# Attention and experts on one core: products with v spread by a table of shares, VectorE's low part of exp read from PSUM, new times for a pair's steps

## The chip, the core and the metric

One NeuronCore of a Trainium2 chip. Times are device microseconds (us) of one execution. TensorE (PE; its weight loads are PEld) multiplies, VectorE (DVE) and ScalarE (ACT) read PSUM and SBUF, GpSimd (POOL) works in SBUF, and SyncE (SP) issues the DMAs. The metric is the median time of a run.

## The reference

```
q_pool = q.reshape(B, H, S // 2, 2, D).mean(axis=3)        # B 2, H 8, S 1152, D 64: 576 pooled queries per head
scores = q_pool @ k^T / sqrt(D);  attn = softmax(scores);  x = attn @ v
out = sum_e p[:, e] * (relu(x @ w1[e]) @ w2[e])            # 1152 rows of 512, 4 experts of 1024
result = ((out @ m1) * (out @ m2)) @ m3 @ mo
```

All in float32. Two outputs of 576 rows and 16 heads in all: 8 pairs of heads.

## The kernel before, in words

**The work of a pair.** Attention goes pair by pair (`i` 0 to 7, heads `s` 0 and 1). For each of the 9 chunks `c` of 128 keys a head takes four score products into a PSUM tile `s` of two banks (L494; two such tiles in all), two passes of exp on ScalarE (L503 `whole`: exp in float32 into an SBUF tile `p`, of which there are four; L510 `hi`: exp in float16 into `ph`), and a subtraction `pl = p - ph`, the low part (`lo`, L515), on GpSimd or VectorE. A head's 135 products with v (`av`, L538 and L540: 5 row blocks, 9 chunks, and ph with v's high part, ph with v's low part, pl with v's high part) run while the next head's scores are made, into one PSUM tile that all heads share. Then `dn` and `x` (L544 to L555) divide and free that tile.

**The next pair's preparation** runs beside it. k is transposed (`kt`, L238; its two parts use the PSUM tiles w0, of two banks, and w1, of one), and cut into `kab` (ScalarE) and `kl` (VectorE). q is pooled on GpSimd (`qp`, L209 and L212), transposed (`qt`, w0) and cut into `qh`, `QZ` and `ql`. For each block of rows a product `mp` (L349, its first two thirds into w0, its last third into w1) and two reductions `mx` on VectorE (L352) find the row maxima: five blocks for head 0, four for head 1. `mf` joins them, `mr` (w1) turns them, `mh` and `ml` cut them, and DMAs place them in the score operand. v gets a scale (`vm`, `vt` in w1, `va` to `vd`, `vs`, `cxp`), and is cut into `vt` high (L470, ScalarE) and low (L474, VectorE). After pairs 3 and 7, `prx` (L464) takes the scale of a whole batch into the experts' shares. The last pair has the first expert's work beside it in place of a next pair's.

**What sets the order.** Every step is put on an agenda with a time written out by hand, and the agenda, sorted, is the order of every engine's instructions. One unit is one chunk; a pair takes 18. The times are offsets in constants at the top: `EX`, `HI`, `LO` for `whole`, `hi` and `lo` after a chunk's scores, `AV0` and `AVN` for the start and length of a head's products with v (spread evenly), `MX0` and `MX1` for the maxima, `KT`, `QT` for the turns of k and q, `TURN` and `ME` for the maxima's turn, `VL` for v's low part, `PQ` for the pooling. An engine runs its instructions in that order, and each waits for what it reads and for the buffer that it writes. PSUM is full: w0 and w1 pass from step to step, so a product waits for the VectorE or ScalarE instruction that read the tile last.

Of the kernel before, what the change touches and what calls it, by code (L numbers as in the profile page):

```python
# [9 lines left out]

TURN = 0.95
KH = 0.15
KL_ = 0.6
QH_ = 0.85
QL_ = 0.5
M0 = 0.4
M1 = 0.05
M2 = 0.6
HI_DVE = (4,)
LO_DVE = ((1, 4), ())  # L20
EX = 0.85
HI = 1.15
LO = 2.1
AV0 = 1.2
AVN = 7.65
VH = 0.5
VL = 3.35
VL0 = -5.5
VR = 4.85
VT = (0.75, 0.8)  # L30
VE = (6.5, 6.75)
PQ = 2.9
PQS = 1.0
WARM = 39
WARM_K = 10
WARM_N = 5
WARM_E = 27
VH0 = 1.5
FIRST = (0.3, 1.4, 2.3, 4.5)
NEAR = 0.0  # L40
LATER = 0
KT = (3, 4)
QT = 5
MX0 = (7, 8, 10, 11, 13)
MX1 = (14, 16, 17, 19)
ME = 0.15
LAST = ((2, 4, 6), (1, 5, 7))
SW = 130
W0 = 123.5
# [14 lines left out]
F32 = mybir.dt.float32  # L64
# [4 lines left out]
AF = mybir.ActivationFunctionType  # L69
ALU = mybir.AluOpType  # L70
# [12 lines left out]
def tile_kernel(ctx: ExitStack, tc: tile.TileContext, q, k, v, dp, w1, w2, mw1, mw2, mw3, mwo, out):  # L83
    nc = tc.nc
    B, H, S, D = q.shape
    P = 128
# [112 lines left out]
    def at(t, f, *args):  # L199
        agenda.append((t, len(agenda), f, args))  # L200
# [281 lines left out]
    def plan_scores(i, s, t):  # L482
        for c in range(NC):
            st = {}

            def pe(c=c, st=st):
                if c == 0:
                    pht[i, s] = ph_p.tile([P, NC, T], F16, tag="ph", name=f"ph{i}_{s}")
                    plt[i, s] = ph_p.tile([P, NC, T], F16, tag="pl", name=f"pl{i}_{s}")
                ps = st["s"] = ps_s.tile([P, 2, 512], F32, tag="s", name=f"s{i}_{s}_{c}")  # L490
                cs = slice(c * P, (c + 1) * P)
                for a, b, first in ((K1, Q1, True), (K2, Q2, False)):
                    for n in range(2):
                        mm(  # L494
                            ps[:, n, :HALF], a[s][:, cs], b[s][:, n * HALF : (n + 1) * HALF],
                            start=first, stop=not first,
                        )

            two = lambda ap: ap.rearrange("p (n t) -> p n t", n=2)

            def whole(c=c, st=st):
                p32 = st["p"] = p32_p.tile([P, T], F32, tag="p32", name=f"p32_{i}_{s}_{c}")
                nc.scalar.activation(out=two(p32), in_=st["s"][:, :, :HALF], func=AF.Exp, scale=SCORE)  # L503

            def hi(c=c, st=st):
                o = pht[i, s][:, c, :]
                if c in HI_DVE:
                    nc.vector.tensor_copy(o, st["p"])
                else:
                    nc.scalar.activation(out=two(o), in_=st["s"][:, :, :HALF], func=AF.Exp, scale=SCORE)  # L510

            def lo(c=c, st=st):
                on_dve = LO_DVE[s] if i < NPAIR - 1 else LAST[s]
                eng = nc.vector if c in on_dve else nc.gpsimd
                eng.tensor_tensor(out=plt[i, s][:, c, :], in0=st["p"], in1=pht[i, s][:, c, :], op=ALU.subtract)  # L515

            at(t + c, pe)
            at(t + c + EX, whole)
            at(t + c + HI, hi)
            at(t + c + LO, lo)  # L520

    def plan_av(i, s, t, span):
        b, h = PAIRS[i]
        xd = slice((h + s) * D, (h + s + 1) * D)
        xo = X[b][:, :, xd]
        st = {}

        def one(j, c, n):
            if (j, c, n) == (0, 0, 0):
                st["t"] = ps_a.tile([P, NB + 1, D + 1], F32, tag="a", name=f"av{i}_{s}")
            o = j * P if j < NB else T - P
            p = (pht, pht, plt)[n][i, s][:, c, o : o + P]
            t = st["t"]
            if n == 1:
                mm(t[:, j, 0:D], p, vt[s][:, c, 0:D], start=False, stop=False)  # L538
            else:
                mm(t[:, j, :], p, vt[s][:, c, D:], start=(c == 0 and n == 0), stop=(c == NC - 1 and n == 2))  # L540

        def out_of():
            dn = tiny.tile([P, NB + 1], F32, tag="dn", name=f"dn{i}_{s}")
            nc.vector.tensor_scalar(  # L544
                out=dn, in0=st["t"][:, :, D], scalar1=PS * EPS, scalar2=vs[i][:, s : s + 1],
                op0=ALU.add, op1=ALU.mult,
            )
            nc.vector.reciprocal(out=dn, in_=dn)
            n = NB if b else NB + 1
            nc.vector.tensor_tensor(  # L550
                out=xo[:, :n], in0=st["t"][:, :n, :D], in1=dn[:, :n].unsqueeze(2).to_broadcast([P, n, D]), op=ALU.mult
            )
            if b:
                r = slice(64, 128)
                nc.vector.tensor_scalar(  # L555
                    out=XT[r, xd], in0=st["t"][r, NB, :D], scalar1=dn[r, NB:], scalar2=None, op0=ALU.mult
                )

        todo = [(j, c, n) for j in range(NB + 1) for c in range(NC) for n in range(3)]
        for k, x in enumerate(todo):  # L560
            at(t + span * k / len(todo), one, *x)
        at(t + span + OUT, out_of)


# [643 lines left out]
```

## Time and profile before

| | |
|---|---|
| median of 3 runs | 877.14 us (876.72 to 877.37) |
| profiled execution | 875.1 us, of which the span from the first to the last instruction is 873.3 us |
| PE busy in the span | 833.9 us, 95% |
| DVE, ACT, POOL busy | 643.4, 406.3, 307.0 us |
| attention after the first half pair (43 to 283 us) | PE 222.2 of 240 us, DVE 204.3, ACT 182.6, POOL 174.5 |

The profile gives one execution. Busy time of an engine is the time in which it has an instruction at work. A gap on PE is put down to the instruction that released it. A time on PE from one group's start to the next group's start is what the group costs there, since matmuls overlap.

### The profile page before, as it was taken

What the parts mean: (1) busy time and instruction counts of PE and PEld (TensorE: products, weight loads), DVE (VectorE), ACT (ScalarE), POOL (GpSimd) and SP (SyncE); (2) the same over time, 40 slices, a digit from 0 to 9 for tenths busy, and PEclk for the clock granted to TensorE, in tenths of its full rate; (3) what the DMA queues carried; (4) which work ended last, traced back from release to release, by engine and by line L of the source; (5) the groups of instructions that cost most, each with busy time, mean ns of one, the idle gap of its engine ahead of it and who ended that gap; (6) DMA issues with size and microseconds to landing.
All of it is one profiled execution on the core that took longest, in us unless ns stands there. A gap on an engine that the chain in (4) does not pass through costs nothing.

```text
span 873.3 us, 16029 instructions
## 1 busy us (share of the span) xinstructions
PE 833.9 (95%) x6388; PEld 597.2 (68%) x6388; DVE 643.4 (74%) x1098; ACT 406.3 (47%) x729; POOL 307.0 (35%) x268
## 2 busy tenths in 40 slices
PE   7799899999889999999999989999999999998998
PEld 5688788888767655555455545555557889988887
DVE  6788988888886566877898988986677865996000
ACT  2677777787685533333344444332214333334111
POOL 4588778777753000000112111101110235667200
PEclk9699999999999999999999999999999999999999
DMA  7666757765440022122222233321110321220011
GB/s 184 161 146 148 173 121 156 163 146 123 112 116 27 25 73 73 51 71 73 73 76 75 92 97 97 97 73 49 49 49 1 107 86 47 78 93 25 13 49 48
DMA packets 59833, 76.74 MB, mean 88 GB/s; under 512 B 23480, under 2 KB 41264, under 8 KB 59760
## 3 DMA queue, kind: packets, MB, share of 16 engines
q1 hardware_dynamic: 59760, 75.73, 32.8%
q8 instruction: 50, 0.82, 0.4%
q14 instruction: 23, 0.19, 0.1%
HBM read 51.92 MB, written 2.36 MB: 62 GB/s over the span
## 4 chain that ended last, share of the span: by engine, by line
PE 64%; DVE 26%; DMA 4%; issue 3%; ACT 1%; SPq 1%; POOL 0%; DVEq 0%; ACTq 0%; POOLq 0%
PE up L678 19%; PE dn L718 18%; PE o L1163 6%; DVE mx L352 5%; PE wf L1115 5%; PE gt L1146 5%; PE s L494 4%; PE mp L349 3%; DVE cv_a L818 2%; DVE vt L474 2%; PE av L540 2%; DVE cv_a L812 2%; DVE cv_a L815 2%; DMA rw<-in_moe_w 1%; DVE w L653 1%
## 5 line engine op out<-in xcount | busy, mean ns | idle before, releaser
L718 PE MATMUL dn<-w,h 128*128 128x512 f16 x840 | 186.4, 379 | 0.0
L515 POOL TENSOR_TENSOR pl<-p,ph 128x576 f16<-128x576 f32 x124 | 164.2, 1338 | 49.2 <-ACT ph L510 38.2
L678 PEld LDWEIGHTS <-w 128*128 128x128 f16 x1152 | 111.7, 98 | 76.0 <-issue 1.6
L718 PEld LDWEIGHTS <-h 128*128 128x128 f16 x840 | 81.6, 98 | 93.2
L684 ACT ACTIVATE up<-up 128x320 f32<-128x320 f32 (+1 forms) x96 | 45.7, 476 | 171.8 <-PE up L678 171.8
L352 DVE TENSOR_REDUCE mx<-mp 128x1 f32<-128x768 f32 (+1 forms) x144 | 101.8, 751 | 21.6 <-PE mp L349 21.2
L494 PE MATMUL s<-Q,K 128*128 128x288 f32 x576 | 113.5, 323 | 2.1 <-ACT ph L510 1.2
L678 PE MATMUL up<-xB,w 128*128 128x320 f16 x768 | 110.5, 299 | 0.6 <-DVE xB L775 0.5
L503 ACT ACTIVATE p<-s 128x576 f32<-128x576 f32 x144 | 93.6, 650 | 34.8 <-PE s L494 29.6
L689 DVE TENSOR_TENSOR h<-up,h 128x320 f16<-128x320 f32 (+1 forms) x94 | 50.8, 551 | 55.8 <-ACT h L685 55.5
L678 PE MATMUL up<-xA,w 128*128 128x512 f16 x384 | 89.1, 379 | 0.6 <-DVE xA L775 0.6
L494 PEld LDWEIGHTS s<-Q,K 128*128 128x128 f32 x576 | 86.6, 198 | 2.8 <-ACT ph L510 1.5
L825 POOL TENSOR_TENSOR cv_x<-cv_x,cv_a 128x512 f32<-128x512 f32 x24 | 30.8, 1284 | 154.3 <-DVE cv_x L822 154.3
L540 PE MATMUL av<-vt,ph 128*128 128x65 f16 x720 | 82.9, 194 | 0.8 <-DVE XT L555 0.6
L540 PE MATMUL av<-vt,pl 128*128 128x65 f16 x720 | 82.9, 196 | 0.2 <-DVE pl L515 0.2
L510 ACT ACTIVATE ph<-s 128x576 f16<-128x576 f32 x128 | 82.6, 645 | 0.0
L538 PE MATMUL av<-vt,ph 128*128 128x64 f16 x720 | 82.2, 194 | 0.0
L825 POOL TENSOR_TENSOR r<-r,cv_a 128x512 f32<-128x512 f32 x16 | 20.4, 1278 | 159.4 <-DVE r L822 159.4
L540 PEld LDWEIGHTS <-ph 128*128 128x128 f16 x720 | 67.1, 99 | 6.9 <-DVE XT L555 1.8
L538 PEld LDWEIGHTS <-ph 128*128 128x128 f16 x720 | 67.0, 97 | 5.7 <-issue 2.3
L540 PEld LDWEIGHTS <-pl 128*128 128x128 f16 x720 | 67.0, 98 | 3.9 <-issue 1.1
L349 PE MATMUL mp<-kab,QZ 128*128 128x384 f32 x216 | 58.3, 377 | 7.4 <-DVE mx L352 4.0
(153 smaller groups left out, 1355.9 us busy)
## 6 DMA issues: line engine op xcount, KB each, us to landing
rw<-in_moe_w SPq DMA_DIRECT2D x64, 512.0 KB
K<-kab SPq DMA_DIRECT2D x32, 288.0 KB
rk<-in_k SPq DMA_DIRECT2D x16, 288.0 KB
rv<-in_v SPq DMA_DIRECT2D x8, 576.0 KB
Q<-qh SPq DMA_DIRECT2D x32, 144.0 KB
K<-kl SPq DMA_DIRECT2D x16, 288.0 KB
rq<-in_q SPq DMA_DIRECT2D x8, 512.0 KB
rw<-in_moe_w_out SPq DMA_DIRECT2D x8, 512.0 KB
```

What stands on the lines that cost most here:

```text
L349: mm(ps[:, n, :PC], QZ[:, o : o + P], KAB[i][:, sl], start=True, stop=True)
L352: nc.vector.tensor_reduce(out=mx[i, s][:, j, g : g + 1], in_=st.pop((j, g))[:, :, :PC], axis=AX.XY, op=ALU.max)
L494: mm(ps[:, n, :HALF], a[s][:, cs], b[s][:, n * HALF : (n + 1) * HALF], start=first, stop=not first,)
L503: nc.scalar.activation(out=two(p32), in_=st["s"][:, :, :HALF], func=AF.Exp, scale=SCORE)
L510: nc.scalar.activation(out=two(o), in_=st["s"][:, :, :HALF], func=AF.Exp, scale=SCORE)
L515: eng.tensor_tensor(out=plt[i, s][:, c, :], in0=st["p"], in1=pht[i, s][:, c, :], op=ALU.subtract)
L538: mm(t[:, j, 0:D], p, vt[s][:, c, 0:D], start=False, stop=False)
L540: mm(t[:, j, :], p, vt[s][:, c, D:], start=(c == 0 and n == 0), stop=(c == NC - 1 and n == 2))
L678: mm(p, w[:, a, c, fc * P : (fc + 1) * P], x[b][:, c, lo - o : hi - o], start=(c == 0 and a == b), stop=(c == KD - 1 and a == 1),)
L718: mm(p, hid[n][a][:, fc, t * P : (t + 1) * P], w[:, b, fc, :], start=(fc == 0 and a == b), stop=(fc == 1 and a == 1),)
L825: nc.gpsimd.tensor_tensor(out=x, in0=x, in1=a.bitcast(F32), op=ALU.add)
L1163: mm(p, gt[c][:, a, t * P : (t + 1) * P], wf[c][:, b, lo:hi], start=(m == 0), stop=(m == 23))
```

## The change

Three things. First, `lo` on VectorE no longer reads `p` from SBUF: for these chunks ScalarE makes `hi` first, then writes float32 exp over the scores in PSUM, and VectorE subtracts from there. These are now chunk 2 of head 0 of a pair (before: chunks 1 and 4), and in the last pair the same chunks as before, 2, 4, 6 and 1, 5, 7. The copy that made `hi` of chunk 4 on VectorE is gone; ScalarE makes it like the others. Second, a head's products with v are spread over its time by a table of shares for eight equal parts of it. Third, nearly all constants have new values.

```diff
-HI_DVE = (4,)
-LO_DVE = ((1, 4), ())
-EX = 0.85
-HI = 1.15
-LO = 2.1
-AV0 = 1.2
-AVN = 7.65
+LO_DVE = ((2,), ())
+EX = 0.49
+HI = 1.01
+LO = 1.19
+LOV = 1.09
+AV0 = 1.09
+AVN = 7.58
+AVW = ((1.0, 0.1, 0.85, 0.35, 1.25, 0.35, 1.15, 2.95), (1.0, 1.5, 0.7, 1.3, 1.5, 0.5, 0.5, 1.0))
...
-VL = 3.35
+VL = 2.56
...
-KT = (3, 4)
+KT = (3.05, 3.05)
...
-            def whole(c=c, st=st):
-                p32 = st["p"] = p32_p.tile([P, T], F32, tag="p32", name=f"p32_{i}_{s}_{c}")
-                nc.scalar.activation(out=two(p32), in_=st["s"][:, :, :HALF], func=AF.Exp, scale=SCORE)
+            on_dve = c in (LO_DVE[s] if i < NPAIR - 1 else LAST[s])
+
+            def whole(c=c, st=st, on_dve=on_dve):
+                x = st["s"][:, :, :HALF]
+                if on_dve:
+                    o = x
+                else:
+                    st["p"] = p32_p.tile([P, T], F32, tag="p32", name=f"p32_{i}_{s}_{c}")
+                    o = two(st["p"])
+                nc.scalar.activation(out=o, in_=x, func=AF.Exp, scale=SCORE)
...
-                if c in HI_DVE:
-                    nc.vector.tensor_copy(o, st["p"])
+                nc.scalar.activation(out=two(o), in_=st["s"][:, :, :HALF], func=AF.Exp, scale=SCORE)
...
+                if on_dve:
+                    nc.vector.tensor_tensor(out=two(o), in0=st["s"][:, :, :HALF], in1=two(h), op=ALU.subtract)
                 else:
...
-            at(t + c + EX, whole)
-            at(t + c + HI, hi)
-            at(t + c + LO, lo)
+            at(t + c + (HI if on_dve else EX), whole)
+            at(t + c + (EX if on_dve else HI), hi)
+            at(t + c + (LOV if on_dve else LO), lo)
...
+        share = AVW[s] if span == AVN else (1,) * 8
+        ends = [sum(share[:n]) / sum(share) for n in range(9)]
         for k, x in enumerate(todo):
-            at(t + span * k / len(todo), one, *x)
+            y = k / len(todo)
+            n = max(m for m in range(8) if ends[m] <= y)
+            at(t + span * (n + (y - ends[n]) / (ends[n + 1] - ends[n])) / 8, one, *x)
```

Three places where it moves instructions. The first is VectorE from the last maxima of pair 4 to the next pair's k, before the change; the numbers in a name are pair, head and step, and the last one counts tiles.

```order
L352 TENSOR_REDUCE mx4_1_2575<-mp4_1_3_1_2734 128x1
L368 TENSOR_REDUCE mf4_1_2773<-mx4_1_2575 128x4
L369 TENSOR_REDUCE mf4_1_2773<-mx4_0_2359 128x1
L515 TENSOR_TENSOR pl4_0_2712<-p32_4_0_1_2759,ph4_0_2711 128x576
L474 SCALAR_TENSOR_TENSOR vt0_120<-rv4_1913,vs4_2345,vt0_120 128x9x64
L393 TENSOR_TENSOR ml4_1_2823<-mr4_1_2811,mh4_1_2817 5x128
L244 TENSOR_TENSOR kl5_2800<-kt5_0_2801,kab5_2799 128x768
```

And the same stretch of VectorE after it.

```order
L353 TENSOR_REDUCE mx4_1_2546<-mp4_1_3_1_2729 128x1
L369 TENSOR_REDUCE mf4_1_2762<-mx4_1_2546 128x4
L370 TENSOR_REDUCE mf4_1_2762<-mx4_0_2365 128x1
L475 SCALAR_TENSOR_TENSOR vt0_120<-rv4_1927,vs4_2357,vt0_120 128x9x64
L520 TENSOR_TENSOR pl4_0_2709<-s4_0_2_2765,ph4_0_2708 128x576
L394 TENSOR_TENSOR ml4_1_2829<-mr4_1_2807,mh4_1_2824 5x128
L245 TENSOR_TENSOR kl5_2810<-kt5_0_2811,kab5_2809 128x768
```

The low part of chunk 1, from SBUF, stood ahead of v's low part; now that of chunk 2, from PSUM, stands behind it, and `ml` still follows both.

The second place is TensorE at the turn of the maxima and of k in the same pair, before; 15 more products with v, the scores of chunk 4 and then `kt5_1` follow.

```order
L494 MATMUL s4_0_3_2794<-Q2_0_128,K2_0_124 128x288 x2
L238 MATMUL kt5_0_2801<-ident_64,rk5_2322 128x128 x6
L540 LDWEIGHTS pl3_1_2424
L540 MATMUL av3_1_2744<-vt1_121,pl3_1_2424 128x65
L540 LDWEIGHTS ph3_1_2423
L540 MATMUL av3_1_2744<-vt1_121,ph3_1_2423 128x65
L385 MATMUL mr4_1_2811<-ident_64,mf4_1_2773 5x128
L538 LDWEIGHTS ph3_1_2423
L538 MATMUL av3_1_2744<-vt1_121,ph3_1_2423 128x64
```

And the same place after.

```order
L495 MATMUL s4_0_3_2801<-Q2_0_128,K2_0_124 128x288 x2
L386 MATMUL mr4_1_2807<-ident_64,mf4_1_2762 5x128
L239 MATMUL kt5_0_2811<-ident_64,rk5_2292 128x128 x6
L239 MATMUL kt5_1_2818<-ident_64,rk5_2292 128x128 x3
L546 LDWEIGHTS ph3_1_2420
L546 MATMUL av3_1_2737<-vt1_121,ph3_1_2420 128x64
```

`kt5_1` writes the tile w1 that `ml4_1` has to read out first. Between `mr4_1` and it stood 16 products with v and the scores of chunk 4; now only `kt5_0` stands there, and those products and the scores come behind it.

The third place is VectorE in the middle of a pair, from the third to the fifth block of the next pair's maxima, before.

```order
L352 TENSOR_REDUCE mx5_0_2969<-mp5_0_2_1_3059 128x1
L352 TENSOR_REDUCE mx5_0_2969<-mp5_0_3_0_3088 128x1
L352 TENSOR_REDUCE mx5_0_2969<-mp5_0_3_1_3091 128x1
L474 SCALAR_TENSOR_TENSOR vt1_121<-rv4_1913,vs4_2345,vt1_121 128x9x64
L352 TENSOR_REDUCE mx5_0_2969<-mp5_0_4_0_3151 128x1
L352 TENSOR_REDUCE mx5_0_2969<-mp5_0_4_1_3154 128x1
L508 CAST ph4_1_3033<-p32_4_1_4_3175 128x576
L366 TENSOR_REDUCE mf5_0_3195<-mx5_0_2969 128x5
```

And after.

```order
L353 TENSOR_REDUCE mx5_0_2974<-mp5_0_2_1_3055 128x1
L475 SCALAR_TENSOR_TENSOR vt1_121<-rv4_1927,vs4_2357,vt1_121 128x9x64
L353 TENSOR_REDUCE mx5_0_2974<-mp5_0_3_0_3093 128x1
L353 TENSOR_REDUCE mx5_0_2974<-mp5_0_3_1_3096 128x1
L353 TENSOR_REDUCE mx5_0_2974<-mp5_0_4_0_3130 128x1
L353 TENSOR_REDUCE mx5_0_2974<-mp5_0_4_1_3133 128x1
L367 TENSOR_REDUCE mf5_0_3164<-mx5_0_2974 128x5
```

v's low part moved ahead of the fourth block's reductions, and the copy of chunk 4 is gone.

## Rows read from the trace of the kernel before

**Rows 1.** Window of the attention: busy us of each engine, granted clock, DMA

```profile
43.00:283.00 240.00, 222.19 (x3065) 192.21 (x3064) 204.33 (x370) 182.62 (x321) 174.46 (x148) 0.99 0.56 131
```

**Rows 2.** Windows by pair, from one pair's first maxima product to the next's

```profile
99.63:131.28 31.65, 28.30 (x387) 24.70 (x387) 28.24 (x51) 23.62 (x43) 24.22 (x22) 1.00 0.62 141
...
160.92:190.58 29.66, 28.12 (x387) 24.61 (x387) 25.72 (x48) 23.71 (x43) 24.34 (x22) 1.00 0.64 150
190.58:220.43 29.85, 28.02 (x387) 24.55 (x387) 25.88 (x49) 23.75 (x43) 24.02 (x22) 1.00 0.59 129
```

**Rows 3.** Waits of PEld in the pair 160.92:190.58: us, times, longest

```profile
PEld kt L238 <- DVE ml L393: 0.9, 1, 0.9
PEld mp L349 <- PE s L494: 0.5, 1, 0.5
PEld vt L425 <- PE av L540: 0.4, 1, 0.4
```

**Rows 4.** The chain through the same pair: start us, us, what

```profile
165.65 0.20 PE av L540
...
165.88 0.06 PE av L540 x2
...
168.70 1.71 DVE vt L474
...
174.33 0.61 PE s L494 x4
174.93 0.53 PE mp L349 x3
...
179.71 1.43 DVE mx L352 x2
...
182.21 2.25 DVE vt L474
184.46 0.21 DVE ml L393
...
184.71 0.56 PE kt L238 x3
```

**Rows 5.** VectorE's groups in that pair: busy us, mean ns, idle before

```profile
L352 DVE TENSOR_REDUCE mx<-mp 128x1 f32<-128x768 f32 x9 | 8.6, 954 | 2.6 <-PE mp L349 2.6
L474 DVE SCALAR_TENSOR_TENSOR vt<-rv,vs,vt 128x576 f16<-128x576 f32 x2 | 4.0, 2020 | 0.0
L515 DVE TENSOR_TENSOR pl<-p,ph 128x576 f16<-128x576 f32 x2 | 1.7, 860 | 0.0
L508 DVE CAST ph<-p 128x576 f16<-128x576 f32 x2 | 0.9, 447 | 0.0
L295 DVE TENSOR_TENSOR ql<-qt,qh 128x576 fp32r<-128x576 f32 x1 | 0.7, 737 | 0.0
```

**Rows 6.** Timeline of ScalarE, the two passes over a chunk: start us, us

```profile
163.00 0.65 ACT L503 ACTIVATE p<-s 128x576 f32<-128x576 f32 x1 [1.04 <-PE s L494]
163.54 0.65 ACT L510 ACTIVATE ph<-s 128x576 f16<-128x576 f32 x1
```

**Rows 7.** Timeline of POOL and PE in the first pair; then a window of PE there

```profile
31.14 1.28 POOL L515 TENSOR_TENSOR pl<-p,ph 128x576 f16<-128x576 f32 x1
...
34.15 1.09 PE L291 MATMUL qt<-ident,qp 128*128 128x128 f32 x4 [1.25 <-POOL pl L515]
...
36.00:38.00 2.00, 1.17 (x5) 0.50 0.91 206
```

**Rows 8.** Timeline of VectorE and PE at the eighth pair's first maxima

```profile
220.87 2.44 DVE L464 TENSOR_SCALAR prx<-pr,cxi 128x16 f32<-128x16 f32 x2
...
224.35 1.15 PE L349 MATMUL mp<-kab,QZ 128*128 128x384 f32 x3 [1.96 <-DVE mx L352]
```

**Rows 9.** Timeline of VectorE and PE in the last pair

```profile
244.31 2.35 DVE L611 TENSOR_REDUCE wm<-rw 128x1 f32<-128x1024 f32 x2
...
246.84 0.28 PE L385 MATMUL mr<-ident,mf 128*5 128x128 f32 x1 [0.84 <-DVE mf L369]
```

More of the change, by code (lines that the diff above doesn't have):

```diff
@@ L9 @@
 from concourse.masks import make_identity
[L11 to L14, printed above, removed]
+TURN = 1.03
+KH = 0.59
+KL_ = 0.22
+QH_ = 0.35
 QL_ = 0.5
-M0 = 0.4
-M1 = 0.05
-M2 = 0.6
-HI_DVE = (4,)
-LO_DVE = ((1, 4), ())
-EX = 0.85
-HI = 1.15
-LO = 2.1
-AV0 = 1.2
-AVN = 7.65
-VH = 0.5
-VL = 3.35
[L28 to L33, printed above, removed]
+M0 = 0.2
+M1 = 0.01
+M2 = 0.39
+LO_DVE = ((2,), ())
[6 more added lines that the diff above has]
+AVW = ((1.0, 0.1, 0.85, 0.35, 1.25, 0.35, 1.15, 2.95), (1.0, 1.5, 0.7, 1.3, 1.5, 0.5, 0.5, 1.0))
+VH = 0.15
+VL = 2.56
+VL0 = -4.21
+VR = 4.92
+VT = (0.27, 0.8)
+VE = (6.01, 6.93)
+PQ = 1.67
+PQS = 1.3
 WARM = 39
@@ L38 @@
 VH0 = 1.5
-FIRST = (0.3, 1.4, 2.3, 4.5)
+FIRST = (0.71, 1.14, 2.3, 4.68)
 NEAR = 0.0
 LATER = 0
-KT = (3, 4)
[L43 to L46, printed above, removed]
+KT = (3.05, 3.05)
+QT = 4.89
+MX0 = (7, 8, 10, 11.72, 13.01)
+MX1 = (14, 16, 17, 18.92)
+ME = 0.07
 LAST = ((2, 4, 6), (1, 5, 7))
@@ L499, in plan_scores, with lo @@
             two = lambda ap: ap.rearrange("p (n t) -> p n t", n=2)
-            def whole(c=c, st=st):
-                p32 = st["p"] = p32_p.tile([P, T], F32, tag="p32", name=f"p32_{i}_{s}_{c}")
-                nc.scalar.activation(out=two(p32), in_=st["s"][:, :, :HALF], func=AF.Exp, scale=SCORE)
+            on_dve = c in (LO_DVE[s] if i < NPAIR - 1 else LAST[s])
[7 more added lines that the diff above has]
+                nc.scalar.activation(out=o, in_=x, func=AF.Exp, scale=SCORE)
             def hi(c=c, st=st):
                 o = pht[i, s][:, c, :]
-                if c in HI_DVE:
-                    nc.vector.tensor_copy(o, st["p"])
-                else:
[L510 to L515, printed above, removed]
+                nc.scalar.activation(out=two(o), in_=st["s"][:, :, :HALF], func=AF.Exp, scale=SCORE)
+            def lo(c=c, st=st, on_dve=on_dve):
+                o, h = plt[i, s][:, c, :], pht[i, s][:, c, :]
+                if on_dve:
+                    nc.vector.tensor_tensor(out=two(o), in0=st["s"][:, :, :HALF], in1=two(h), op=ALU.subtract)
+                else:
+                    nc.gpsimd.tensor_tensor(out=o, in0=st["p"], in1=h, op=ALU.subtract)
             at(t + c, pe)
-            at(t + c + EX, whole)
-            at(t + c + HI, hi)
-            at(t + c + LO, lo)
+            at(t + c + (HI if on_dve else EX), whole)
+            at(t + c + (EX if on_dve else HI), hi)
+            at(t + c + (LOV if on_dve else LO), lo)
     def plan_av(i, s, t, span):
```

## The prediction

> **What bounds the kernel now.** I read the window of the attention first, then those by pair, then the waits of one pair and the chain through it. In the first the reader is to see that TensorE is the busiest engine, but that in the attention it stands idle for 17.8 us of 240 (240 - 222.2) [rows 1]. The experts' work behind it keeps its instructions and their order, so what can move lies in the attention and the start: at most some 18 us, 2%.
>
> The windows by pair give the period: 29.66 us in the first batch, 29.85 in the second, and 31.65 where `prx` falls [rows 2]. Within a period TensorE waits several times, and nearly always for VectorE: 0.9 us at `kt` for `ml`, 0.4 at `vt`, 0.5 at the first maxima product (put down to PE; what comes late there is `cxp`, which frees w1) [rows 3]. VectorE is busy for 25.72 of 29.66 us, ScalarE for 23.71, GpSimd for 24.34 [rows 2]. The chain shows the same: from 179.71 to the second part of `kt` at 184.71 it stays on VectorE, through reductions, `pl`, 2.25 us of v's low part and `ml` [rows 4]. So a pair is bound by TensorE and VectorE in turns, and TensorE's own work does not change. The question is which of its waits go and which come.
>
> **The change, part by part.**
>
> *VectorE's work.* Per pair it loses two copies of 0.447 and two low parts of 0.860 from SBUF, and gains one low part with one operand in PSUM [rows 5]: no row shows that form. The nearest is `ql`, the same subtraction of 576 columns with PSUM as first operand, at 0.737; the other end is the SBUF form's 0.860. I take 0.74, or 0.7 from start to start. VectorE loses 2.61 - 0.74 = 1.9 us per pair. [...]
>
> *ScalarE and GpSimd.* ScalarE makes `hi` of chunk 4 in both heads: two more passes of 0.65 per pair [rows 6], 25.0 of 29; no row shows exp written into PSUM, and I price it like the same pass into SBUF. GpSimd makes 17 low parts instead of 16, at 1.28 [rows 7]: 25.6 of 29. Both have over 5 us idle per pair now [rows 2], and that idle time hides them, so they cost nothing. Without that cover, ScalarE's 1.3 us would go onto each pair.
>
> *The tile held longer.* Chunk 2's PSUM tile is now freed by VectorE, not ScalarE, and the scores of chunk 4 want it. On TensorE those scores come behind `kt`'s second part, which waits for `ml`, and `ml` stands behind this low part on VectorE. So the hold costs nothing of its own. What stands behind it is `ml`, and that is counted below.
>
> *The order of a pair.* I split the period 160.92 to 190.58 at two events: the head's first product with v at 165.65, and `kt`'s second part at 184.71 [rows 4]. That makes 4.73 + 19.06 + 5.87 us.
>
> First part, now 4.73: VectorE does two blocks of maxima (1.43 each) and then `dn` to `x`. TensorE comes to the second block 6 products earlier (12 instead of 18, 0.03 each), but its tile is only free when the first reduction (0.954) is over [rows 5]. I count 0.1 off (0 to 0.2).
>
> Second part, now 19.06. TensorE's own work is 135 products at 0.03 = 4.1, eight scores at 0.61 = 4.9, five maxima products at 0.53 = 2.65, and `mr`, one small product, at 0.1 by estimate: 11.7 us to the last maxima product [rows 4]. Waits come on top: v's low part (1.71) now stands ahead of the fourth block's reductions, and fewer products lie between the blocks (15 and 8, before 35 and 18). TensorE therefore waits about 0.4 at the fifth block and 0.4 at the first of the other head: 12.5. Before, VectorE began the last block's reductions 14.06 after the part's start (179.71 - 165.65); now it is 12.5 + 0.55 for the product = 13.05, because 35 products instead of 14 lie between the last two blocks, and `dn` to `x` fit there. From there: reductions 1.43, `mf` 0.2, v's low part 2.25, `pl` 0.7, `ml` to `kt` 0.25 [rows 4] = 4.85, `pl` being the price above. Sum 17.9, so 1.15 off. v's low part took 1.71 and 2.25 in this one pair, so it has those two prices; I take the long one, as it is the one in this place. With 1.71 another 0.5 goes. In the second batch `x` has a further instruction for the odd rows, which puts back some 0.4; over three pairs of each batch that is 0.2. So 0.95 off (0.4 to 1.5).
>
> Third part, now 5.87, of which 0.9 are waits at `vt` and at the first maxima product [rows 3], both behind the copy, the second low part and their neighbours on VectorE. These have left this place, so I count the waits as gone: 5.0 us of work. The scores of chunk 4 (0.61) and 16 products (0.5) come into this part from the second: 6.1, so 0.2 more.
>
> Together 0.1 + 0.95 - 0.2 = 0.85 off per pair, times six periods, from the first maxima product of the second pair's scores to that of the eighth's: 5.1 us.
>
> *The stretch of prx.* TensorE waits 1.96 us there at the eighth pair's maxima, and about as long at the fourth's, in the period that is 2 us longer than the others [rows 2, 8]. `prx` waits on nothing that moves: 0 (0.5 either way for each).
>
> *The start.* `qt` of the second pair began at 34.15 after 1.25 us of waiting [rows 7]. Its tile is freed by a reduction that stood behind `vm` on VectorE and now stands ahead of it; the pooled q now comes behind two low parts on GpSimd (1.28 each) instead of one. About 1 us earlier, of which I keep 0.5, since the later turns here wait for other steps (0 to 1).
>
> *The last pair.* `mr` waited 0.84 us because `mf` stood behind two reductions of the expert's weights (2.35) [rows 9]. Now `mf` stands ahead: 0.84 off. Against it, two low parts that wait for ScalarE move up among the expert's first steps; for it, the last one moves out of the way of `wa`. I count 0.8 off (2 off to 1 more).
>
> Sum: 5.1 + 0.5 + 0.8 = 6.4. The profiled execution took 875.1 us (span 873.3 and 1.8 around it), 2.0 less than the median of the runs, 877.14. 875.1 - 6.4 = 868.7 on its scale, **870.7 us** as a median.
>
> **The rivals.**
>
> *The waits only move (no change).* The new waits in the middle of a pair are twice what I count and `kt` waits longer, 0.7 per pair in all. For it: the table of shares puts fewer products between the maxima there, though VectorE needs 1.43 per block. Against it: VectorE has 1.9 us less to do. Then 0.15 per pair and the smaller terms stay: 0.9 + 1.3 = 2.2 off, 874.9, and with those at nothing 876.2.
>
> *Slower: the low part from PSUM holds up `ml`.* Place: between v's low part and `ml` on VectorE. It waits for ScalarE's second pass over chunk 2. ScalarE has v's high part and six passes to do from the end of the head's products on, some 0.8 + 6 x 0.54 = 4.0 us, as two passes start 0.54 apart [rows 6]; VectorE comes to it 4.4 us after the last maxima product (0.55 + 1.43 + 0.2 + 2.25), and the products end 0.6 before that. So ScalarE has about a microsecond in hand. Beyond that each microsecond of delay goes onto `kt` and each of six pairs, as only `kt`'s first part (0.6) is left between `mr` and it. The gain is gone at 6.4 / 6 = 1.1 us of delay behind the spare one; at 1.6 the time is 877.1 + 3.2 = 880.3. For it: ScalarE is in order, and v's high part waits for the products' end. Against it: it has 6 us idle per pair.
>
> *More than I count.* v's low part at 1.71 in every place, and TensorE's clock, which was granted at 0.50 (1.2 GHz) in 36 to 38 us [rows 7] after waits, back at full earlier: 6 x 0.5 + 2.5 more, 865.2.
>
> **How the numbers follow.** My sum with its spread, 866.5 to 875, has 0.60; the moved waits (about 875 to 877.5) 0.17; slower as described 0.10; more than I count 0.13. A difference below 0.2% (1.75 us) is about what a measurement of this kernel cannot tell from none. The range from 864.5 to 877 leaves out the slower case, a little of the moved waits and the far end of the last: under 0.2. Faster by over 0.2% (below 875.4): 0.60 + 0.13 and a part of the second case, 0.77. Same: 0.13. Slower: 0.10.
>
> **What would show it.** Right: a period of about 28.8 us in the windows by pair; VectorE's busy time per pair down by about 1.9; no wait at `vt` and at the first maxima product; `mr` of the last pair without its 0.84; the low part from PSUM at about 0.74. Still there: a wait of `kt` for `ml` of some 0.7, and new ones of the fifth block for `mx`. Wrong: periods of 29.5 or more, with `kt` waiting over 1.5 us, or VectorE idle in front of the low part for ScalarE.

## The result, and the profile after

The changed kernel takes 862.36 us (median of 4 runs, 861.34 to 865.90) against 876.93 for the kernel before (4 runs). The ratio is 0.9844, 95% interval 0.9813 to 0.9875: faster by 1.6%, some 14 us. The sign was right, the size was not: 870.7 was forecast, and the time lies below the range. The profiled execution of after is the slowest of its four, 865.9 (span 864.1): its granted clock was 0.988, as in the profiled execution of before, and 0.992 to 0.996 in the other three.

The windows by pair of the kernel after, and the window of the attention (columns as in [rows 1]):

```profile
94.76:123.69 28.93, 27.68 (x389) 24.47 (x388) 23.87 (x46) 24.66 (x45) 25.07 (x23) 1.00 0.67 155
151.58:179.46 27.88, 27.59 (x390) 24.50 (x388) 22.24 (x44) 24.56 (x45) 25.07 (x23) 1.00 0.69 162
179.46:208.30 28.84, 27.85 (x390) 24.50 (x388) 23.64 (x47) 24.56 (x45) 24.97 (x23) 1.00 0.58 135
43.00:274.00 231.00, 221.17 (x3064) 190.85 (x3064) 180.66 (x349) 188.49 (x334) 177.11 (x153) 0.99 0.57 134
```

Beside [rows 2], the ordinary pair fell from 29.66 to 27.88 us. TensorE is busy in 27.59 of it, so TensorE's own work now fills nearly all of an ordinary pair. VectorE lost 3.5 us of busy time per pair (25.72 to 22.24), where 1.9 were forecast: that surplus is the first sign of what was missed. The waits of PEld in that pair, beside [rows 3]:

```profile
PEld mp L350 <- DVE mx L353: 0.6, 3, 0.2
...
PEld kt L239 <- DVE ml L394: 0.4, 1, 0.4
PEld L548 <- DVE x L558: 0.4, 1, 0.4
```

The waits at `vt` and at the first maxima product are gone, that of `kt` is 0.4 instead of 0.9, and what is left comes in pieces of 0.2. VectorE's groups in the pair, beside [rows 5] (busy us, mean ns):

```profile
L475 DVE SCALAR_TENSOR_TENSOR vt<-rv,vs,vt 128x576 f16<-128x576 f32 x2 | 1.9, 954 | 0.0
...
L520 DVE TENSOR_TENSOR pl<-s,ph 128x576 f16<-128x576 f32 x1 | 0.8, 757 | 0.2 <-issue 0.2
```

The subtraction from PSUM takes 0.757, as priced (0.74). But v's low part, an instruction that the change does not edit, fell from a mean of 2020 ns to 954. The timeline of VectorE in this pair, at the last maxima (the place of 179.71 to 184.71 in [rows 4]):

```profile
169.47 1.43 DVE L353 TENSOR_REDUCE mx<-mp 128x1 f32<-128x768 f32 x2
...
171.07 0.98 DVE L475 SCALAR_TENSOR_TENSOR vt<-rv,vs,vt 128x576 f16<-128x576 f32 x1
172.28 0.76 DVE L520 TENSOR_TENSOR pl<-s,ph 128x576 f16<-128x576 f32 x1 [0.23 <-issue]
172.95 0.27 DVE L394 TENSOR_TENSOR ml<-mr,mh 5x128 f32<-5x128 f32 x1
```

and of TensorE, at the head's first product with v and at the second part of `kt`:

```profile
156.17 0.20 PE L548 MATMUL av<-vt,ph 128*128 128x65 f16 x1
...
173.28 0.55 PE L239 MATMUL kt<-ident,rk 128*128 128x128 f32 x3 [0.19 <-DVE ml L394]
```

From the last maxima to `kt` it took 3.81 us (169.47 to 173.28), before 5.00.

What GpSimd did in the meantime accounts for it; the runs further down test that. First the kernel before, VectorE at the 2.25 of [rows 4], then GpSimd:

```profile
181.31 0.98 DVE L515 TENSOR_TENSOR pl<-p,ph 128x576 f16<-128x576 f32 x1
182.21 2.25 DVE L474 SCALAR_TENSOR_TENSOR vt<-rv,vs,vt 128x576 f16<-128x576 f32 x1
...
180.38 1.29 POOL L515 TENSOR_TENSOR pl<-p,ph 128x576 f16<-128x576 f32 x1
181.62 0.98 POOL L212 TENSOR_TENSOR qp<-rt 64x128 f32<-64x128 f32 x1
182.56 1.27 POOL L515 TENSOR_TENSOR pl<-p,ph 128x576 f16<-128x576 f32 x1
```

then GpSimd after:

```profile
170.15 1.29 POOL L522 TENSOR_TENSOR pl<-p,ph 128x576 f16<-128x576 f32 x1 [0.98 <-ACT ph L515]
171.40 1.25 POOL L210 TENSOR_TENSOR qp<-rq 128x256 f32<-128x256 f32 x1
172.61 1.28 POOL L522 TENSOR_TENSOR pl<-p,ph 128x576 f16<-128x576 f32 x1
```

Read the ends. Before, VectorE's `pl` ends 0.62 behind the end of GpSimd's `pl` (182.29 and 181.67). GpSimd's `qp` then takes 0.98, where it takes 0.45 in e7 (below), with nothing in its way. v's low part ends 0.63 behind the next GpSimd `pl` (184.46 and 183.83). After, v's low part ends at 172.05, 0.61 behind GpSimd's `pl` (171.44), and it is GpSimd's `qp` that waits (1.25 instead of 0.73). So GpSimd and these VectorE instructions, both with two SBUF inputs, keep each other waiting here. VectorE's ends 0.61 to 0.63 after GpSimd's is through, and that in all 34 places of the two traces where v's low part or a `pl` from SBUF took over 0.9 us on VectorE; GpSimd's `qp` ended 0.31 and 0.60 after VectorE's. This wait is called a hold from here on.

### The profile page after: what moved, and what is told of

The parts are those of the page before. It is cut to its first block, busy times and chain, and to the rows that moved or that the text cites. A ratio compares the mean times of both kernels' runs of the same rounds, so it can differ in the third digit from the quotient of the medians.

```text
span 864.1 us, 16020 instructions
## 1 busy us (share of the span) xinstructions
PE 832.9 (96%) x6388; PEld 595.0 (69%) x6388; DVE 617.8 (72%) x1075; ACT 413.7 (48%) x745; POOL 311.5 (36%) x275
## 4 chain that ended last, share of the span: by engine, by line
PE 71%; DVE 18%; ACT 4%; DMA 3%; issue 3%; SPq 0%; POOL 0%; DVEq 0%; ACTq 0%; POOLq 0%
PE up L691 19%; PE dn L731 18%; PE s L495 6%; PE o L1176 6%; PE wf L1128 5%; PE gt L1159 5%; PE av L548 4%; PE mp L350 3%; DVE mx L353 3%; DVE cv_a L831 2%; PE av L546 2%; DVE cv_a L825 2%; DVE cv_a L828 2%; DMA rw<-in_moe_w 1%; DVE w L666 1%
## 5 line engine op out<-in xcount | busy, mean ns | idle before, releaser
L522 POOL TENSOR_TENSOR pl<-p,ph 128x576 f16<-128x576 f32 x131 | 169.2, 1310 | 55.7 <-ACT ph L515 50.8
L495 PE MATMUL s<-Q,K 128*128 128x288 f32 x576 | 111.5, 319 | 3.6 <-ACT ph L515 2.3
L511 ACT ACTIVATE p<-s 128x576 f32<-128x576 f32 x131 | 84.8, 647 | 19.7 <-PE s L495 17.5
L515 ACT ACTIVATE ph<-s 128x576 f16<-128x576 f32 x144 | 91.7, 647 | 0.0
L548 PE MATMUL av<-vt,ph 128*128 128x65 f16 x720 | 81.1, 193 | 1.2 <-DVE XT L563 0.8
```

The lines of the kernel that those rows point to most:

```text
L495: mm(ps[:, n, :HALF], a[s][:, cs], b[s][:, n * HALF : (n + 1) * HALF], start=first, stop=not first,)
L511: nc.scalar.activation(out=o, in_=x, func=AF.Exp, scale=SCORE)
L522: nc.gpsimd.tensor_tensor(out=o, in0=st["p"], in1=h, op=ALU.subtract)
```

## The experiments

My theory, **Hold**: the time came from GpSimd keeping VectorE less. Its rivals: **Work** (VectorE simply has less to do) and **Order** or **Times** (TensorE's order, the new agenda). The table sets whole times beside a finer measure, the six periods from the first maxima product of the second pair's scores to that of the eighth's (start to start on TensorE, in the profiled execution). It leaves out the start and the last pair, where the clock differed between executions (from 30 to 44 us it was granted at 0.63 in before, 0.76 in after and 1.00 in e11, from 210 to 260 at 0.97, 0.93 and 1.00). The first of the six periods is still touched by the clock: after and e4 have the same instructions in all six, and differ by 0.53 us in the first (29.36 at a granted clock of 0.94, 28.83 at 1.00) and by 0.02 at most in each other. In e6 the clock fell in the third period too (0.75 from 100 to 102 us, 0.50 from 102 to 104). So a difference below some 0.6 us says nothing here. Without the first period before takes 150.5 us and after 141.4. "GpSimd cut" is explained at e7.

| kernel | us (median) | ratio to before, 95% | six periods, us |
|---|---|---|---|
| before | 876.93 | 1 | 39.80 to 220.46: 180.66 |
| after | 862.36 | 0.9844 (0.9813 to 0.9875) | 37.52 to 208.30: 170.78 |
| e6 new times alone | 870.57 | 0.9940 (0.9924 to 0.9956) | 177.21 |
| e2 new division of work alone | 868.43 | 0.9909 (0.9892 to 0.9926) | 173.10 |
| e1 both, even shares | 864.09 | 0.9865 (0.9846 to 0.9883) | 172.60 |
| e3 after, low part from SBUF | 863.10 | 0.9851 (0.9832 to 0.9869) | 172.24 |
| e7 before, GpSimd cut | 862.77 | 0.9855 (0.9833 to 0.9877) | 173.05 |
| e12 new times alone, GpSimd cut | 862.96 | 0.9858 (0.9840 to 0.9875) | 171.39 |
| e13 new work alone, GpSimd cut | 862.92 | 0.9856 (0.9842 to 0.9870) | 170.37 |
| e14 both, even shares, GpSimd cut | 859.66 | 0.9821 (0.9801 to 0.9842) | 170.49 |
| e11 after, GpSimd cut | 854.61 | 0.9759 (0.9744 to 0.9775) | 167.88 |
| e15 before, v's low part first | 877.03 | 1.0015 (1.0005 to 1.0025) | 181.96 |
| e8 after, v's low part twice | 883.26 | 1.0080 (1.0063 to 1.0097) | 184.54 |
| e9 after, second one later | 866.68 | 0.9888 (0.9866 to 0.9909) | 172.26 |
| e5 after, v's low part later | 864.20 | 0.9862 (0.9841 to 0.9882) | 173.06 |
| e4 after, last pair from SBUF | 862.41 | 0.9848 (0.9827 to 0.9869) | 170.26 |
| e10 after, prx later | 861.00 | 0.9833 (0.9817 to 0.9849) | 169.21 |
| f1 e4, e10 and one more move | 860.48 | 0.9827 (0.9812 to 0.9842) | 169.90 |

**Parts of the change (e1, e2, e3, e6).** e1 is after with

```diff
-AVW = ((1.0, 0.1, 0.85, 0.35, 1.25, 0.35, 1.15, 2.95), (1.0, 1.5, 0.7, 1.3, 1.5, 0.5, 0.5, 1.0))
+AVW = ((1,) * 8, (1,) * 8)
```

> The kernel after, with the products with v spread evenly again (every share 1); all else as after. Hold (the time came from VectorE's v low part and prx being kept less by GpSimd): the table does not touch VectorE's or GpSimd's order, so the v low parts stay at 0.9 to 1.35 us, the periods of ordinary pairs within 0.3 us of 27.9, and the whole within 2 us of after's 862.4. Order (the time came from where TensorE does its products): the waits at the first maxima product and at vt come back, periods 28.6 to 29.6, the whole 868 to 874. Work (less work on VectorE is what paid): within 1 us of after.

e2 is that with all the old constants and `LOV = 1.25`:

> The kernel before with the low-part change alone: all old times, even shares, but chunk 2's low part on VectorE from PSUM, chunks 1 and 4 to GpSimd, no copy of chunk 4 on VectorE. Work: VectorE has about 2 us less a pair, so most of the gain is here, 864 to 868, ordinary periods about 28.2. Order: old order, old waits, 873 to 878. Hold: decided by what GpSimd runs beside v's low part, which the old times set; with GpSimd taking two chunks more it is busier there, so v's low part of the first head stays at 1.7 to 2.3 us and the whole at 870 to 877; if the trace shows it under 1.35 instead, the whole should be under 868.

e3 is after with

```diff
-                if on_dve:
-                    nc.vector.tensor_tensor(out=two(o), in0=st["s"][:, :, :HALF], in1=two(h), op=ALU.subtract)
+                eng = nc.vector if on_dve else nc.gpsimd
+                eng.tensor_tensor(out=o, in0=st["p"], in1=h, op=ALU.subtract)
```

with `whole` writing `p` in SBUF for these chunks too.

> The kernel after with the PSUM part undone: chunk 2's low part (and the last pair's chunks of LAST) stays on VectorE but reads the copy of p in SBUF, with ScalarE's two passes kept in after's order for these chunks. Hold: an instruction with two SBUF inputs more on VectorE, which GpSimd can keep: it takes 0.73 to 1.9 us instead of 0.76, and moves v's low part behind it only if they are neighbours; 0 to 0.4 us a pair, whole 862 to 866. Work: the same instruction count, whole within 1 us of after. Order: within 1 us of after in the pairs. All three: the last pair's TensorE waits for tiles of scores held by VectorE's low part are unchanged or lower, since the tile is read by ScalarE alone: up to 2 us less there.

and e6 is before with the new constants:

> The kernel before with all new times but the old division of work: low parts of chunks 1 and 4 on VectorE from SBUF, chunk 4's copy on VectorE, even shares. Order or re-timing: the gain is in the times, so the whole is 862 to 867 and periods 27.9 to 28.5. Work: VectorE's old work is back (28.0 to 28.2 busy at 954 ns a maxima pass and 860 ns a low part, of a period of 28), the whole 870 to 877. Hold: the three instructions put back are of the kind that GpSimd keeps (0.86 on average where 0.73 is the least): v's low part is between 0.9 and 2.3 by what stands beside it, the whole 864 to 872.

No part has it all. The division of work alone brings 7.6 us in the six periods, the times alone 3.5, both 8.1, and the uneven shares another 1.8. In e1 v's low part stayed short (0.87 to 1.20 in most places) and the periods rose to 28.2, the edge of what Hold allowed: the shares pay a little by themselves. e3 costs 1.5 us in the six periods: where the one low part left to VectorE is read from matters less than that the other one and two copies went. e3's low part from SBUF was held a little (1.02 to 1.04, from PSUM 0.76). By their whole times e2 and e6 decide nothing between Hold and Work: e6 lies in the spans of both, e2 just above Work's. Hold's own number for e2, 870 to 877 with v's low part of the first head at 1.7 or more, was wrong: it fell to 0.92 to 1.22 (1.28 in e6, before 2.25), for which Hold had set a whole under 868 (868.43 came), while that of the other head stayed at up to 1.83 in both. In e1, Work's "within 1 us of after" and Order's 868 to 874 were missed.

**GpSimd cut in before (e7).** Low parts of GpSimd over 16 columns only; the products read the high part instead, so those low parts are missing from the result:

```diff
-                eng.tensor_tensor(out=plt[i, s][:, c, :], in0=st["p"], in1=pht[i, s][:, c, :], op=ALU.subtract)
+                n = T if eng is nc.vector else 16
+                eng.tensor_tensor(out=plt[i, s][:, c, :n], in0=st["p"][:, :n], in1=pht[i, s][:, c, :n], op=ALU.subtract)
```

> The kernel before with GpSimd's low parts cut to 16 of 576 columns; the products with v that would read these low parts read the high parts instead, so the result leaves the low parts of those chunks out. Same instructions on every engine in the same order; VectorE's own work is as before. Hold: v's low part falls from 1.7 to 2.25 us to 0.8 to 1.3 in all pairs, the low parts and prx shorten too, and with it the time: 866 to 870, ordinary periods 27.9 to 28.7. Work: VectorE still has 28 us of work to do of kinds whose least time is known (pl 0.73, ph 0.45, mx 0.955), so little is gained: 873 to 877. Order: TensorE's order is as before and the waits are in it: 874 to 878.

862.77, below Hold's 866 to 870 and far from the others' spans: as fast as after, with before's order and VectorE's old work. VectorE's timeline there, at the place of the 2.25:

```profile
172.90 0.75 DVE L516 TENSOR_TENSOR pl<-p,ph 128x576 f16<-128x576 f32 x1
173.56 0.81 DVE L474 SCALAR_TENSOR_TENSOR vt<-rv,vs,vt 128x576 f16<-128x576 f32 x1
175.40 0.28 DVE L393 TENSOR_TENSOR ml<-mr,mh 5x128 f32<-5x128 f32 x1 [1.03 <-ACT mh L389]
```

v's low part is held nowhere now (0.81 or 0.82 in all sixteen places), and `ml` even waits for ScalarE. So the holds cost before about as much as the change wins, and neither Work nor Order foretold that. The cut could also have shortened plain waits for GpSimd's results. From 40 to 218 us of before there were few: none of TensorE, and two of ScalarE of 1.05 and 1.04 us. What fell there were TensorE's waits for VectorE, on PEld from 6.3 to 1.9 us at `kt` for `ml`, and from 4.2 to 2.1 at `mp` for `mx`. But the ordinary pair, by the windows of e7, came down by 1.0 of the 1.8 only:

```profile
124.14:152.77 28.63, 27.85 (x388) 24.59 (x388) 22.97 (x46) 23.54 (x43) 6.94 (x21) 1.00 0.68 157
```

**GpSimd cut elsewhere (e11, e12, e13, e14),** the same edit in after, e6, e2 and e1.

> The kernel after with GpSimd's low parts cut to 16 of 576 columns, as was done to the kernel before (the products with v read the high parts in their place, so the result leaves those low parts out). Hold as the whole story: with GpSimd out of the way before took 862.8; after, where GpSimd keeps VectorE little, gains little from it: ordinary pairs 27.6 to 27.9, the whole 858 to 862, most of it from prx. If re-timing and the share table are worth as much without GpSimd's holds as the 5.8 us that new times alone gave: 856 to 858, 5 us or more under before's kernel with the same cut. If they only avoid holds: 862 to 863, the same as before's kernel with the same cut.

> All new times with the old division of work and even shares (870.6 us with GpSimd's low parts), and GpSimd's low parts cut to 16 of 576 columns, the products with v reading high parts in their place. Times as what is left of the gain when nothing is held: 855 to 858, ordinary periods 27.9 to 28.1, near the kernel after with the same cut (854.6). Work as what is left: near the kernel before with the same cut, 861 to 863, periods 28.4 to 28.7.

> All old times and even shares with the new division of work (868.4 us with GpSimd's low parts), and the same cut of GpSimd's. Work as what is left of the gain when nothing is held: 855 to 858, periods 27.9 to 28.1. Times as what is left: 861 to 863, periods 28.4 to 28.7, as before's kernel with the same cut.

> The kernel after with even shares and the same cut of GpSimd's. If the uneven shares are worth 0.3 us a pair by TensorE's own order: periods 28.1 to 28.2 and 856 to 857. If they only paid with GpSimd's holds in place: 27.9 and within 1 us of 854.6.

The windows of e11, an ordinary pair and the one that took 28.84 in after:

```profile
148.19:176.05 27.86, 27.61 (x390) 24.50 (x388) 21.95 (x44) 24.54 (x45) 7.39 (x22) 1.00 0.69 161
176.05:204.17 28.12, 27.59 (x389) 24.48 (x388) 22.58 (x47) 24.55 (x45) 6.83 (x22) 1.00 0.61 140
```

In the ordinary pair of after GpSimd costs nothing any more (27.88 and 27.86); where v's low part is still held, at 1.71, it costs 0.7 (28.84 and 28.12). The six periods can be summed: GpSimd's low parts cost before 7.6 us (180.66 - 173.05) and after 2.9 (170.78 - 167.88), so 4.7 of the 9.9 us are holds avoided. The other 5.2 (173.05 - 167.88) remain with almost nothing held (v's low part at 0.81 to 0.96 in e11): 2.7 come with the division of work (e13), the new times add nothing to that (e14), and the shares 2.6 (e14 to e11). Without the first period the sums are alike: 4.6 of 9.0 avoided, and of the other 4.5 the division of work 2.7 and the shares 2.1. In another order of the parts the split differs (the times alone bring 1.7, e12). Expected was that times or work alone would bring e12 or e13 to 855 to 858; both stayed at 863, as e7, so neither is what is left by itself. e11's 854.61 lies below all that was expected of it, e14's 859.66 above. The whole times are blurred by the clock. These windows of e11, of a stretch at the start, one with the last pair, and one among the experts, have the granted clock third from the right:

```profile
30.00:44.00 14.00, 10.99 (x88) 8.59 (x89) 11.37 (x27) 10.77 (x21) 4.01 (x13) 1.00 0.59 143
210.00:260.00 50.00, 45.80 (x677) 38.13 (x677) 35.63 (x70) 38.12 (x66) 4.99 (x20) 1.00 0.35 87
500.00:516.00 16.00, 16.00 (x85) 8.12 (x83) 14.38 (x22) 4.90 (x8) 1.27 (x1) 1.00 0.38 103
```

and of after:

```profile
30.00:44.00 14.00, 10.10 (x57) 8.50 (x56) 9.81 (x24) 9.71 (x18) 12.43 (x13) 0.76 0.59 137
210.00:260.00 50.00, 44.18 (x526) 35.50 (x526) 36.06 (x65) 37.97 (x66) 27.43 (x21) 0.93 0.41 99
500.00:516.00 16.00, 12.72 (x61) 6.20 (x60) 13.14 (x26) 5.89 (x10) 2.32 (x2) 0.89 0.19 62
```

Taking the missing share of the clock as lost, that is, as an estimate from these windows, 14 x 0.24 + 50 x 0.07 + 16 x 0.11 = 8.6 us of their 11.1 us of span, at most. So e11's whole time overstates what holds still cost in after.

**Where the hold goes (e15).** Before with one constant changed:

```diff
-VL = 3.35
+VL = 2.56
```

> The kernel before with one constant changed: v's low part at 2.56 of the agenda for 3.35, which puts it ahead of the low part of chunk 1 on VectorE in place of behind it (the same work in the same stretch ahead of the cut of the row), and one half block earlier at the other head. Hold: who is kept waiting changes with the place, so v's low part of the first head falls from 2.25 to 1.0 to 1.4 us and the low part behind it may grow; the whole 868 to 874. Work or order alone: the same two instructions in either order ahead of the cut, no change, 875 to 877.

VectorE's timeline of e15:

```profile
181.25 1.01 DVE L474 SCALAR_TENSOR_TENSOR vt<-rv,vs,vt 128x576 f16<-128x576 f32 x1
182.18 2.25 DVE L515 TENSOR_TENSOR pl<-p,ph 128x576 f16<-128x576 f32 x1
184.35 0.27 DVE L393 TENSOR_TENSOR ml<-mr,mh 5x128 f32<-5x128 f32 x1
```

As Hold had it, v's low part fell to 1.01; but the 2.25 went to the low part of exp behind it, `ml` begins when it did, and the whole is 0.15% slower. So the hold is not the instruction's, and its place alone wins nothing: these two instructions in a row pay it between them. My number for the whole (868 to 874) was wrong for that reason, and the rival's "no change" was nearly right (877.03, its span was 875 to 877): only the trace shows the hold. With the second one's input in PSUM, as in after, it is not paid there (0.76). But two in a row need not pay as much: in e3 the second, from SBUF too, took 1.03.

**A dose, and its place (e8, e9, e5).** After with a second v low part, straight behind the first (e8), or behind `ml` (e9):

```diff
                 at(t + 9 * s + VL, v_lo, i, s)
+                at(t + 9 * s + VL, v_lo, i, s)
```

> The kernel after with v's low part done twice, one straight behind the other, in each head of each pair. Hold (v's low part is on the chain there: maxima, v's low part, low part of exp, cut of the maxima's row, TensorE's spread of k): 0.8 to 1.3 us more ahead of the cut of the row of each pair, half of it covered by the 0.3 us that TensorE idles now and none at the other head: 0.5 to 1.3 us a pair, whole 866 to 871. Bound by TensorE alone (VectorE has 5 us idle in a pair of 27.9, so it hides): within 1.5 us of after, 861 to 864.

> The kernel after with the same second v low part, put behind the cut of the maxima's row of each head, where VectorE idles 0.65 to 0.76 us now. Hold: off the chain, so 0 to 0.3 us a pair: 862 to 865, 3 us or more under the kernel with the second one straight behind the first. Work: VectorE's work grows by as much as there, so the two kernels cost the same within 1 us.

e8 costs 2.4 us a pair (30.23), nearly twice the most that was expected: held at 1.17 and 1.73, the second one makes TensorE wait at both heads, in the waits of PEld of e8's pair

```profile
PEld mp L350 <- DVE mx L353: 1.9, 4, 1.4
PEld kt L239 <- DVE ml L394: 1.3, 1, 1.3
```

e9, with the same instruction elsewhere, costs 0.25 a pair (28.14), as expected, though its whole time, 866.68, is above the 862 to 865 that was expected. So VectorE's time counts in the stretches ahead of `ml` and of the maxima, and hardly elsewhere. e5 moves v's low part (`VL = 3.4`) behind `ml` at the first head and behind the fourth block at the other:

> The kernel after with v's low part at 3.4 of the agenda in place of 2.56: at the first head it now stands behind the low part of exp and behind the cut of the maxima's row, at the other head behind the fourth block of maxima. Hold: 1.0 us less ahead of the cut, so TensorE's 0.4 us wait at the spread of k goes, and at most 0.4 us a pair is won: 859 to 863. Work: the same work, so 861 to 864. A rival of its own: beside another GpSimd instruction it is held longer in the new place (1.7 to 2.2 us, to be read in its rows) but hidden there.

It lost 2.3 us in the six periods, and its 864.20 is above the 859 to 863 that was expected: held at 1.42 in the new place of the other head, it makes the fifth block wait 0.53, and the pair takes 28.4. At the first head it took 0.83 in most places, almost free, and won nothing.

**The last pair (e4), prx (e10), and all together (f1).** In e4 the low parts of the eighth pair read SBUF again.

> The kernel after, but in the eighth pair the low parts of the chunks of LAST on VectorE read the copy of p in SBUF, with ScalarE's passes in the order copy, high part, as before. If VectorE's low part from PSUM is what holds the tiles of scores there (TensorE waits 1.02, 1.23 and 1.27 us for them in the profile of after, 1.27 of it for VectorE's low part): the wait of 1.27 goes and the whole is 1 to 2 us less, 860 to 861.5. Rival: ScalarE's two passes hold the tiles (1.2 us waits stay, now for ScalarE) and the whole is within 1 us of after; a kernel with all low parts of VectorE from SBUF again showed 1.23 and 0.47 there, which speaks for something between.

No change (862.41 and 862.36; the executions of each spread over some 4 us): as its rival had it. TensorE's waits in after's last pair, then in e4's:

```profile
232.69 0.79 PE L495 MATMUL s<-Q,K 128*128 128x288 f32 x4 [1.02 <-ACT ph L515]
...
240.61 0.80 PE L495 MATMUL s<-Q,K 128*128 128x288 f32 x4 [1.23 <-ACT ph L515]
...
243.06 1.33 PE L495 MATMUL s<-Q,K 128*128 128x288 f32 x4 [1.27 <-DVE pl L520]
```

```profile
234.62 0.66 PE L763 MATMUL xt<-ident,x 128*128 128x128 f32 x4 [2.68 <-DVE ml L394]
...
241.30 0.79 PE L495 MATMUL s<-Q,K 128*128 128x288 f32 x4 [1.24 <-ACT ph L516]
...
242.96 0.90 PE L495 MATMUL s<-Q,K 128*128 128x288 f32 x4 [0.48 <-ACT ph L516]
```

The wait for VectorE's low part went (1.27 to 0.48 for ScalarE), and 2.68 came at `xt`, which waits for `ml`. e10:

```diff
-            if n == NPAIR // B - 1:
-                at_rows(b)
...
+        if i % (NPAIR // B) == NPAIR // B - 1:
+            at(te + 8.55, at_rows, i // (NPAIR // B))
```

> The kernel after with the reciprocal and the two prx instructions of each half moved 8.5 steps of the agenda later, behind the cut of the maxima's row of the next pair's first head, where VectorE idles 0.65 us. Hold: prx (1.3 us of its 1.6 are a wait for GpSimd) is what makes the two pairs with it 1.0 us longer than the ordinary ones: both fall to 27.9 to 28.2, the whole by 1.0 to 2.0 us against after, 860.4 to 861.4. Rival: prx is as long there and now keeps the other head's maxima back: the same 1 us a pair, no change.

The second `prx` in after, and both in e10 on VectorE:

```profile
208.77 1.24 DVE L465 TENSOR_SCALAR prx<-pr,cxi 64x4 f32<-64x4 f32 x1
```

```profile
221.32 0.48 DVE L465 TENSOR_SCALAR prx<-pr,cxi 128x16 f32<-128x16 f32 x2
```

The second one, of four columns, took 1.24 us, behind GpSimd; in the new place both together take 0.48. The period with the first pair of them fell from 28.93 to 27.89, that of its neighbours.

> The kernel after with three things together: the eighth pair's low parts on VectorE from SBUF, prx later, and v's low part of each pair's first head at 3.4, behind the low part of exp and the cut of the row (the other head's stays). Hold: 1 to 2 us from the two prx pairs, 0 to 1.3 in the eighth pair, and up to 0.3 a pair from TensorE's wait at the spread of k: 858 to 861. Rival (TensorE alone bounds it, 27.6 of 27.9 us): only prx pays, 860.5 to 862.

f1 is under both kernels, 860.48. Against after its interval overlaps, so that it beats after is likely, not shown.

## Why the prediction was wrong

**The step that failed** in the sum is in the second part of a pair: "v's low part took 1.71 and 2.25 in this one pair, so it has those two prices; I take the long one, as it is the one in this place." Neither is a price (and the 1.71 is the chain's part of an instruction of 1.79). It is 0.81 of work (e7) and a wait for GpSimd, and it measured 0.98 there. Split at the same events, the pair 151.58 to 179.46 gives:

- first part, to the product at 156.17: 4.59, off by 0.14 (forecast 0.1);
- second, to `kt` at 173.28: 17.11, off by 1.95 (forecast 0.95);
- third, to 179.46: 6.18, longer by 0.31 (forecast 0.2).

Within the second, the last block's reductions begin 13.30 after the first product (forecast 13.05: the waits put in for the shares were about right). The stretch behind them takes 3.81 instead of 4.85. The rest of the mechanism stood: waits at `vt` and the first maxima product gone, low part from PSUM at 0.757, `kt` still waiting, ScalarE and GpSimd hidden (24.56 and 25.07 of 27.88).

**The step to the median** failed beside it. The forecast took the median 2.0 above the profiled execution, as before's was (868.7 to 870.7), so it put a change of the clock at nothing. After's profiled execution took 865.9, 2.8 below the 868.7; its median lies another 3.5 below that. The four executions of after took 865.9, 863.0, 861.7 and 861.3 at granted clocks of 0.988, 0.992, 0.996 and 0.996; those of before that were measured beside e1 had 0.982 to 0.992. So of the 14.6 us between the medians 5.4 lie between the profiled executions and the medians, and after's 3.5 of them go with the clock. What decides over the clock was not tried apart.

**The six periods** gave 9.9 us instead of 5.1. Half is holds avoided (4.7), shown by cutting GpSimd in both kernels. That the change avoided them by taking low parts and copies off VectorE, and not by moving v's low part, is what e15 (moved alone: nothing) and e2 say together: with work alone the six periods came down by 7.6, and cutting GpSimd there too won only 2.7 more (173.10 to 170.37, e13), where it won 7.6 in before.

**prx**, forecast at 0 because it "waits on nothing that moves", waited for GpSimd (0.22 to 0.24 in e7 for each of its instructions, 1.24 here): the period with it lost 2.72 where its neighbours lost 1.8 (31.65 to 28.93), since one of its two instructions was no longer held (at the eighth pair 0.32 and 1.24 us, before 2.44 together [rows 8]); e10 shows what was left.

**The start**, forecast at 0.5: 2.3 (first maxima product at 37.52, before at 39.80). In e7, with the old order and GpSimd cut, it is at 37.83. But the clock differed there: from 30 to 44 us it was granted at 0.63 in before, 0.76 in after and 0.88 in e7. How much of the 2.3 is the clock, how much GpSimd, and which step of the change won it, was not tried apart.

**The last pair**, forecast at 0.8 off: from the eighth pair's first maxima product to the end the profiled executions took 2.95 longer (655.8 and 652.8 us). `mr` lost its 0.84, as forecast, but TensorE waits for tiles of scores and at `xt`, 4.0 us in four places (1.02, 0.48, 1.23, 1.27), before 3.5 in five. Behind those waits the clock fell. By the windows above, 50 x 0.07 + 16 x 0.11 = 5.3 us of clock are missing in after from there on by estimate, and in before 50 x 0.03 = 1.5 (0.97 from 210 to 260, 1.00 from 500 to 516): the difference can be all of the 2.95. Its size in the median is open. e4 shows that the tile held in PSUM is not what decides there.

The sum over the profiled executions, -9.9 - 2.3 + 2.95, is the difference of the spans (873.3 to 864.1). The medians are 14.6 apart, since after's profiled execution was 3.5 above its median and before's 1.8 under its own of four runs. Of the rivals, "more than I count" (865.2) had the right places, v's low part and the clock, and took 1.71 for the least where 0.81 is. "The waits only move" and "slower" did not happen: VectorE waits 0.23 ahead of the low part from PSUM, and `kt` less than before.

## What to carry to other kernels

A duration that varies between equal instructions (1.71, 2.25, 0.81) can hold a wait for another engine, as here: lay the other engine's ends beside its own end before using it as a price. Where GpSimd works beside VectorE, count the VectorE instructions with two SBUF inputs in each critical stretch (here one took up to 2.25 us for 0.81 of work); give one of them an input in PSUM (0.76 here, never held) or move it out, for reordering them only passed the wait on here (e15). And measure repeated work by its period, with the granted clock beside each period, when the clock makes executions differ by as much as the effect; a forecast of the median needs a term for the clock.

## What the runs showed of the hardware that was not expected

- An instruction of VectorE with two SBUF inputs that GpSimd kept waiting ended 0.61 to 0.63 us after GpSimd's, in all 34 places. One instruction of VectorE waited out the ends of two of GpSimd's (2.25 for 0.81 of work, begun at 182.21, over ends at 182.60 and 183.83).
- The subtraction with one input in PSUM was not held: 0.757 beside a GpSimd that was busy for 25.07 of 27.88 us, and 0.735 to 0.759 in all 13 places of after. With nothing held, the form from SBUF took 0.746 (mean in e7), 11 ns less.
- `prx`, a `tensor_scalar` of 16 or 4 columns with one SBUF tensor and one value per row, is kept too: 1.24 or 1.33 us held, 0.22 to 0.24 free (e7). Held, it ends 0.02 to 0.03 after GpSimd's `pl`, where the instructions of 576 columns end 0.61 to 0.63 after. Why an instruction with one SBUF tensor is kept was not shown.
- In after the granted clock fell behind TensorE's waits of 1.23 and 1.27 us in the last pair (0.61, 0.50, 0.50 and 0.68 in the windows from 242 to 250), but waits alone do not say when: in e5 TensorE was busy for only 1.58 of the 4 us from 240 to 244, in after for 2.12, and the clock of e5 stayed at 1.00 from 240 to 256. At 0.50 a product of 512 columns took TensorE 0.43 us from start to start in after (244.19 to 245.49 for three), at 1.00 0.216 (598.77 to 601.36 for twelve): some 1.2 and 2.4 columns per ns.
